# One table of numbers replaced: a second searched order for a fused S4D convolution and Hedgehog attention kernel

## The chip, the core and the metric

The kernel runs on one core of one Trainium2 chip. The metric is the time of one execution in device microseconds (us), as the median of several runs.

## The reference

Two independent layers read their own inputs, and their outputs stand side by side in a (1, 2048, 1152) result. All numbers are float32.

```python
# A: S4D, L=2048, D=576, N=128
dt = exp(log_dt);  A = -exp(log_A_real) + 1j * A_imag
C = (C_real + 1j * C_imag) * dt[:, None]
K = 2 * einsum("dn,dnl->dl", C, exp((A * dt[:, None])[:, :, None] * pos)).real
y = irfft(rfft(u_t, 2 * L) * rfft(K, 2 * L))[:, :, :L]
a = y.transpose(0, 2, 1) + u * D_skip

# B: linear attention, H=32 heads of 18
q, k, v = split(x @ wqkv)
phi = lambda t: concat(softmax(t @ w_phi), softmax(-(t @ w_phi)))     # per head
kv = einsum("bhsf,bhsd->bhfd", phi(k), v);  z = phi(k).sum(s)
o = (phi(q) @ kv) / (phi(q) @ z + 1e-6)
b = o.reshape(B, S, D) @ wo

return concatenate([a, b], axis=-1)
```

## The kernel before

**How the program is put together.** The function `body` does not emit instructions directly. It records 2836 operations through `Plan.op` (a load, a run of matmuls, a copy, an exp, and so on), each with its engine, the operations that it depends on and the buffers that it opens. Then `Plan.run` walks a literal table, `ORDER`, and emits the operations one after another in the order of that table. An entry such as `1250/0/1/7/2/2` says: emit operation 1250 next, and give the buffers that it opens the slots 0, 1, 7, 2 and 2 of their kinds. A star (`268*`) sends an operation that two engines could do to the second of them, and an exclamation mark loads an activation table ahead of need. `7+28` puts 28 filler matmuls at the start. The waits between the engines follow from the table: every engine executes its own instructions in the order in which they were emitted; an operation waits for what it reads and for the earlier readers of a slot that it overwrites. So the table sets two things besides the engine of some operations: who stands behind whom on each engine, and which earlier operation has to be finished before a buffer can be filled again.

**Which buffers there are.** Fourteen large slots serve `zi`, `ac`, `e`, `ks`, `E`; nineteen row slots serve, among others, `ub`, `kb`, `zo`, `fT`, `ot`; there are eight PSUM slots `ps`. All loads and stores that are spoken of below are issued by SP, in order, so that a load which waits for its slot holds back every load and store behind it.

**The work of part B.** All large products run as three products of a high and a low half of the float32 operands (`wh`, `wl` for weights, `x` for tiles). First `fold` multiplies the key weights with the per-head `w_phi`: it loads a block of transposed weights (`e<-in_wkT_dram`, L504) and the `w_phi` block (`fT<-in_wphi_dram`, L500), TensorE multiplies them, ACT writes the high half (`wh<-ps`, L515) and DVE the low half (`wl`, L516). Sixteen key tiles follow (product with `wh`/`wl`, two softmaxes, accumulation of phi(k)ᵀ[v, 1] in the matmuls `ps<-e,v`). Between the last key tiles the same `fold` is done for the query weights (`e<-in_wqT_dram`), of which the first product of a query tile needs every block. Sixteen query tiles then take their softmax, turn the features with nine transposes (`ps<-ident,e`, L701), multiply with kv (`ps<-kvb,fT`) and divide, turn the result (`ps<-ident,o`, L731 and L732) and multiply it with `wo`.

**The work of part A**, interleaved with it. `u_first` does the first stage of the transform of u, 16 times, and stores it (`dram<-zi`, 576 KB). `params` (L845 and after) turns the parameters into exponents and phases in six blocks: its activations need the exp table for `dt<-dt` and the table of the arctangent for `ax<-mn`, and POOL adds integer phases (`pi`, L886). 36 groups build K: products with `sel,mg`, an exp on ACT (L946), products with sines on DVE and POOL (`E`, `cs`, L904, L950 to L956), and 32 small matmuls `ps<-E,cs`. `k_first` stores the first stage of K's transform (`dram<-zi` L989). Sixteen times `product` loads a part of both transforms (`ub<-dram` L1038, `kb<-dram` L1057, a matrix `ff` L1030), makes the products `ub,ff`, `kb,ff` and `ac,ff` on TensorE and stores `zo`; a last stage loads it again as `zi` and makes y.

**The lines in the order's rows and in the trace.** A helper records many operations: L448 is the call of a matmul, L463 and L467 are two-operand operations, L453 a copy. So they are told apart by their tiles. The table is one line shorter after the change, so each line behind it has a number smaller by one there (L448 is L447).

## Time and profile before

| | |
|---|---|
| runs of the kernel before | 512.74, 503.32, 510.81 us; median 510.81 us |
| the profiled execution | 507.23 us; its span 505.4 us |
| instructions in the span | 20522 |
| PE (TensorE matmul) busy | 482.6 us, 95% |
| PEld (TensorE weight load) busy | 404.6 us, 80% |
| DVE, ACT, POOL busy | 454.6 us, 394.9 us, 340.0 us |
| data moved | 115.45 MB, mean 228 GB/s |

The profiled execution is a run of its own, and its 507.23 us lie 1.83 us over the span from its first to its last instruction. A row of the page's groups reads: line, engine, operation, output<-inputs, shapes and count, then the busy time, the mean time of one in ns, and the idle time of the engine ahead of it with what ended it. A row of a timeline reads: start, duration, engine, line, operation, tiles, count, and in brackets how long the engine had been idle ahead of it and what released it. Float32 matmuls count twice in the trace's rows: five of the program stand as x10.

### The profile page before, as it was taken

To read this page: it belongs to the slowest core of one execution; us is meant where nothing else is said; L and a number is where in the kernel's file an instruction comes from. 1 tells how busy PE (TensorE), PEld (TensorE's weight loads), DVE (VectorE), ACT (ScalarE), POOL (GpSimd) and SP (SyncE) were. 2 spreads that over 40 slices of the span, in tenths; PEclk is the share of its full clock that TensorE was granted. 3 is DMA by queue.
4 is the path that set the end of the run, shared out by engine and by line. 5 is a ranking of instruction groups with operands and counts; after the bars stand their busy time and mean duration, and the time that the engine had idled before them with its cause. 6 is when DMAs were issued, how large, how long until landed. Compare 5 with 4: busy or idle time off the path is not lost.

```text
span 505.4 us, 20522 instructions
## 1 busy us (share of the span) xinstructions
PE 482.6 (95%) x8544; PEld 404.6 (80%) x8544; DVE 454.6 (90%) x1010; ACT 394.9 (78%) x684; POOL 340.0 (67%) x413
## 2 busy tenths in 40 slices
PE   6999999999999979899999999998999999998997
PEld 6999988999988768688796877775798786666976
DVE  3999999999999998999998999999898798887684
ACT  5799887999999989998999798999894634444321
POOL 1855789697979996896894799876556327374200
PEclk8999999999999999999999999999999999999999
DMA  8979944822427775567689627878877998999788
GB/s 218 389 239 304 325 146 144 225 81 86 170 69 222 215 237 155 125 217 226 173 270 364 204 67 246 259 242 270 276 251 229 297 291 277 295 284 287 250 303 209
DMA packets 80800, 115.45 MB, mean 228 GB/s; under 512 B 12612, under 2 KB 58564, under 8 KB 80708
## 3 DMA queue, kind: packets, MB, share of 16 engines
q1 hardware_dynamic: 80708, 114.14, 72.2%
q8 instruction: 67, 1.10, 0.9%
q14 instruction: 25, 0.20, 0.1%
HBM read 65.11 MB, written 49.01 MB: 226 GB/s over the span
## 4 chain that ended last, share of the span: by engine, by line
PE 69%; DVE 15%; issue 4%; DMA 4%; POOL 3%; ACT 2%; SPq 1%; DVEq 0%; POOLq 0%; ACTq 0%
PE ps L448 65%; PE ps L701 3%; DVE cs L950 2%; DVE E L467 2%; POOL cs L904 2%; PE ps L731 1%; DVE E L956 1%; DMA kb<-dram 1%; DMA gd<-cs 1%; DVE x L463 1%; DVE E L954 1%; DVE ac L467 1%; DMA ub<-in_wkT_dram 1%; DMA mg<-gd 1%; DVE e L467 1%
## 5 line engine op out<-in xcount | busy, mean ns | idle before, releaser
L448 PE MATMUL ps<-wh,x 128*128 128x288 f32 (+2 forms) x1008 | 241.9, 320 | 0.9 <-DVE e L467 0.4
L448 PEld LDWEIGHTS ps<-wh,x 128*128 128x128 f32 x1008 | 173.4, 188 | 13.2 <-issue 4.8
L448 PE MATMUL ps<-wl,x 128*128 128x288 f32 (+2 forms) x560 | 175.2, 314 | 0.0
L448 PEld LDWEIGHTS ps<-wl,x 128*128 128x128 f32 x560 | 105.5, 188 | 0.2
L904 POOL TENSOR_TENSOR cs<-cs,pi 128x64 int32<-128x64 int32 (+4 forms) x90 | 91.1, 1012 | 4.7
L597 POOL TENSOR_TENSOR o<-e 128x576 f32<-128x576 f32 x32 | 43.0, 1345 | 20.8 <-ACT e L594 16.2
L463 POOL TENSOR_TENSOR E<-v,cs 128x512 f32<-128x512 f32 x34 | 43.6, 1302 | 19.8 <-ACT v L946 19.8
L946 ACT ACTIVATE ps<-ps 128x512 f32<-128x512 f32 x90 | 49.8, 586 | 5.0 <-PE ps L448 4.3
L467 DVE TENSOR_TENSOR ac<-us,ps 128x576 f32<-128x576 f32 x64 | 44.9, 746 | 4.4 <-PE ps L448 2.6
L950 DVE TENSOR_TENSOR cs<-ps,cs 128x1024 f32<-128x1024 f32 x36 | 43.6, 1213 | 1.6 <-ACT ps L946 1.6
L448 PEld LDWEIGHTS ps<-E,cs 128*32 128x32 f32 x2304 | 34.1, 110 | 8.6 <-issue 3.5
L463 POOL TENSOR_TENSOR e<-e,small 128x576 f32<-128x576 f32 x27 | 32.5, 1208 | 12.2 <-DVE small L463 9.5
L922 ACT ACTIVATE cs<-cs,hp 128x1024 f32<-128x1024 f32 x36 | 40.5, 1144 | 0.1
L448 PE MATMUL ps<-E,cs 128*32 128x64 f32 x2304 | 39.2, 220 | 0.9 <-issue 0.4
L594 ACT ACTIVATE e<-e 128x1152 f32<-128x1152 f32 x32 | 37.3, 1167 | 2.6 <-DVE e L463 1.9
L921 ACT ACTIVATE cs<-cs 128x1024 f32<-128x1024 int32 x36 | 37.3, 1054 | 0.2
L886 POOL TENSOR_TENSOR pi<-pi 128x192 int32<-128x192 int32 (+1 forms) x42 | 20.2, 494 | 24.3 <-DVE pi L882 20.2
L463 POOL TENSOR_TENSOR ac<-ac 128x288 f32<-128x288 f32 x31 | 24.2, 808 | 17.5 <-DVE ac L467 17.0
L463 POOL TENSOR_TENSOR e<-small,e 128x576 f32<-128x576 f32 x24 | 28.2, 1174 | 10.7 <-DVE e L467 9.8
L914 ACT ACTIVATE cs<-cs 128x2048 f32<-128x2048 int32 x18 | 34.6, 1922 | 0.5 <-POOL cs L904 0.5
L453 ACT ACTIVATE zi<-ps 128x288 f32<-128x288 f32 x80 | 28.9, 413 | 5.3 <-PE ps L448 5.0
L587 DVE TENSOR_REDUCE small<-ps 128x16 f32<-128x288 f32 (+2 forms) x64 | 28.2, 443 | 4.0 <-PE ps L448 3.7
(143 smaller groups left out, 1013.3 us busy)
## 6 DMA issues: line engine op xcount, KB each, us to landing
dram<-zi SPq DMA_DIRECT2D x32, 288.0 KB, 3.9
xd<-x SPq DMA_DIRECT2D x16, 576.0 KB, 4.1
dram<-zi SPq DMA_DIRECT2D x16, 576.0 KB, 5.6
x<-xd SPq DMA_DIRECT2D x16, 576.0 KB, 4.1
kb<-dram SPq DMA_DIRECT2D x32, 288.0 KB, 4.5
ub<-dram SPq DMA_DIRECT2D x32, 288.0 KB, 4.6
dram<-zo SPq DMA_DIRECT2D x32, 288.0 KB, 4.2
zi<-dram SPq DMA_DIRECT2D x16, 576.0 KB, 7.7
```

Of the source, the lines that this page charges most:

```text
L448: pe.matmul(o, l, r, start=start, stop=stop, skip_group_check=skip)
L453: op(("act", "dve"), (c_act(n), c_dve(n)), lambda e: act.activation(dst(), src(), AF.Copy) if e == "act" else dve.tensor_copy(dst(), src() ...
L463: op(eng, [c_dve(n[0]) if e == "dve" else c_pool(n[1]) for e in eng], lambda e: (dve if e == "dve" else pool).tensor_tensor(dst(), a(), b( ...
L467: op(eng, c_dve(n) if eng == "dve" else c_pool(n), lambda: e.tensor_tensor(dst(), a(), b(), op=alu), r=r, w=w, with_=with_, lock=eng == "p ...
L594: op("act", c_act(1152) + 40, lambda: act.activation(e.t, e.t, AF.Exp), r=[e], w=[e], table="exp")
L597: op("pool", c_pool(517), lambda: pool.tensor_tensor(pair.t, e.t[:, :, :, 0:9], e.t[:, :, :, 9:18], op=ALU.add), r=[e], w=[pair], lock=True)
L904: op("pool", c_add(4 * n * W), lambda n=n, j=j: pool.tensor_tensor(x()[:, :, :, n:2 * n], x()[:, :, :, 0:n], pi.t[:, j:j + 2, gs].bitcast( ...
L914: op(("act", "dve"), (c_act(n) + 45, c_dve(n)), lambda e: act.activation(cs.t[:, 0], x(), AF.Abs) if e == "act" else dve.scalar_tensor_ten ...
L921: op("act", c_act(64 * W) + 150, lambda at=at: act.activation(at(1), at(1).bitcast(I32), AF.Sin, scale=TURN), r=[cs], w=[sine], with_=[cs] ...
L922: op("act", c_act(64 * W) + 225, lambda at=at: act.activation(at(0), at(0), AF.Sin, scale=-TURN, bias=hp.t), r=[cs, hp, sine], w=[both], w ...
L946: op("act", c_act(512) + 12, lambda x=x, y=y: act.activation(y.t, x.t, AF.Exp), r=[x], w=[y], table="exp")
L950: op("dve", c_dve(64 * W), lambda: dve.tensor_tensor(F(), both(M.t), F(), op=ALU.mult), r=[M, ready], w=[long], with_=[cs])
```

## The change

Only the table `ORDER` is different: the same 2836 operations with the same buffers, in another sequence and with other slots, and with some operations on the other of their two engines. Its first two rows:

```diff
-0/0 1 2 234/0 1349 4/1 288/2 1354 1358 1357 1362 1356 1361 1363/3 5/0 7+28/0 1364 1365 1366 1367 1368 1369 1370 6/1
-1355 1359/0 99/4 1371 1360 369/5 1373 1372 19/6 21/2 1374 1375/3 1376 396/7 1377 1378 10 20/3 49/4 12/1 1379 374/8 11
+49/0 5/0 3 0/1 1 2 153/0 1357 1356 4/1 7+28/1 1362 1373 6/2 33 1361 1363/2 1365 1364 1366 1367 1368 72/3 1369 1370
+12/1 1354 1358 35/3 1355 1371 374/4 1372 1359/0 34/4 19/5 1360 1374 14/5 13/6 10 11 369/6 375/1 1375/2 1376 21/1 376*
```

Of the 414 operations that TensorE has, 229 stand at the same place of its sequence, and none moved by more than 15 places. 253 operations run on the second of their engines, before and after. There are 43 loads of an activation table in both, and 376 DMA issues.

**The start, on ACT.** The instructions of the first block of `params` (`dt`, `ay`, `ax`, `pi`), and the first copies of the fold (`wh<-ps`) and of the first tile (`x_193`). Before:

```order
L845 ACT_TABLE_LOAD
L845 ACTIVATE dt<-dt 128x96
L845 ACTIVATE ay<-cim 128x96
L845 ACTIVATE ax<-cre 128x96
L845 ACT_TABLE_LOAD
L845 ACTIVATE ax<-mn 128x96
L845 ACTIVATE ax<-ax 128x96
L861 ACTIVATE pi<-pi 128x96
L845 ACTIVATE ax<-ax 128x96
L515 ACTIVATE wh<-ps 128x126
L543 ACTIVATE x_193<-zo 128x640
```

And now:

```order
L844 ACT_TABLE_LOAD
L844 ACTIVATE ay<-cim 128x96
L844 ACTIVATE ax<-cre 128x96
L844 ACT_TABLE_LOAD
L844 ACTIVATE ax<-mn 128x96
L844 ACTIVATE ax<-ax 128x96
L844 ACT_TABLE_LOAD
L844 ACTIVATE dt<-dt 128x96
L844 ACTIVATE ax<-ax 128x96
L860 ACTIVATE pi<-pi 128x96
L514 ACTIVATE wh<-ps 128x126
L542 ACTIVATE x_193<-zo 128x640
```

The exponential of `dt` and a third table load now stand between the arctangent (`ax<-mn`) and the first copy of the folded weights. On SP the loads of the start changed places too: the first key weights (`e<-in_wkT_dram`) were the fifth load and are the first, `fT<-in_wphi_dram` was the first and is the fourth, and `dt` was the second and is the seventh.

**The fold of the query weights, on PE.** `fT,e` are the fold's products, `sel,mg` and `E,cs` belong to the groups of K, `e,v` accumulates a key tile (its number is that of the tile's `v`). Before:

```order
L448 MATMUL ps<-sel,mg 128x256 x6
L448 MATMUL ps<-e,v_2509 19x36 x32
L448 MATMUL ps<-fT,e 128x126 x8
L448 MATMUL ps<-e,v_2715 19x36 x32
L448 MATMUL ps<-sel,mg 128x256 x6
L448 MATMUL ps<-fT,e 128x126 x5
L448 MATMUL ps<-E,cs 32x64 x32
```

And now:

```order
L447 MATMUL ps<-sel,mg 128x256 x6
L447 MATMUL ps<-e,v_2178 19x36 x32
L447 MATMUL ps<-fT,e 128x126 x5
L447 MATMUL ps<-sel,mg 128x256 x6
L447 MATMUL ps<-e,v_1523 19x36 x32
L447 MATMUL ps<-fT,e 128x126 x9
L447 MATMUL ps<-E,cs 32x64 x32
```

Before, the fourth block of query weights (operation 518, `e<-in_wqT_dram`) was loaded into a slot whose last reader stood seven operations ahead of its product on PE. Now it is loaded into the slot that the `fT,e ... x5` above has just read, and its product is in the `fT,e ... x9`, with a `sel,mg`, an `e,v` and the five products of the third block between them. On SP, the loads around it, before:

```order
L774 DMA dram<-zi 64x1152
L504 DMA e<-in_wqT_dram 126x640
L989 DMA dram<-zi 128x8x144
L491 DMA e<-in_wo_dram 128x960
L504 DMA e<-in_wqT_dram 126x640
L989 DMA dram<-zi 128x8x144
L504 DMA e<-in_wqT_dram 126x640
L554 DMA x_3273<-xd 128x1152
```

And now:

```order
L773 DMA dram<-zi 64x1152
L503 DMA e<-in_wqT_dram 126x640
L838 DMA dt<-in_ldt_dram 128x96
L503 DMA e<-in_wqT_dram 126x640
L988 DMA dram<-zi 128x8x144
L490 DMA e<-in_wo_dram 128x960
L503 DMA e<-in_wqT_dram 126x640 x2
L553 DMA x_3286<-xd 128x1152
```

The third and the fourth block (operations 511 and 518) are issued one behind the other, where a store stood between them. The slot of the third was last read by the 576 KB store of a `k_first` (L988 here).

**The transposes of query tile 9, on PE.** `ident,o` turns that tile's divided output, `ident,e` turns the features of another tile, `ub,ff` and `ac,ff` are of a `product`, `kvb,fT` of a query tile. Before:

```order
L448 MATMUL ps<-ub,ff 32x288 x16
L701 MATMUL ps<-ident,e 128x128 x5
L448 MATMUL ps<-sel,mg 128x256 x6
L701 MATMUL ps<-ident,e 128x128 x4
L731 MATMUL ps<-ident,o 128x128 x4
L732 MATMUL ps<-ident,o 128x128
L448 MATMUL ps<-ac,ff 32x288 x32
```

And now:

```order
L447 MATMUL ps<-ub,ff 32x288 x16
L730 MATMUL ps<-ident,o 128x128 x4
L731 MATMUL ps<-ident,o 128x128
L700 MATMUL ps<-ident,e 128x128 x4
L447 MATMUL ps<-sel,mg 128x256 x6
L700 MATMUL ps<-ident,e 128x128 x4
L447 MATMUL ps<-kvb,fT 64x76 x4
```

The turn of the output went ahead of the other tile's turns and of the group's `sel,mg`; products `kvb,fT` went ahead of `ac,ff`.

**Two smaller places.** Ahead of the first query tile's transposes, three phase adds (`pi`, L886) on POOL went out from in front of the multiplication `e<-e,small` (L463) of that tile. And for `product` 15 the second of the two loads of `kb` (L1057, operations 2706 and 2707) waits for the reader of another slot: before, for the product `kb,ff` of `product` 10, now for its product `ub,ff`, which stands one operation earlier on PE.

## The prediction

> **What bounds the kernel now.** I read the page's busy times first, then TensorE's own waits, then the windows around the largest of them. The page's first part, and the two rows of its chain and groups that bear on the bound:

> ```profile
> span 505.4 us, 20522 instructions
> PE 482.6 (95%) x8544; PEld 404.6 (80%) x8544; DVE 454.6 (90%) x1010; ACT 394.9 (78%) x684; POOL 340.0 (67%) x413
> PE 69%; DVE 15%; issue 4%; DMA 4%; POOL 3%; ACT 2%; SPq 1%; DVEq 0%; POOLq 0%; ACTq 0%
> L448 PE MATMUL ps<-wh,x 128*128 128x288 f32 (+2 forms) x1008 | 241.9, 320 | 0.9 <-DVE e L467 0.4
> ```

> TensorE is busy for 482.6 us of 505.4, so 22.8 us of idle time are all that another order can take from it as long as its matmuls cost the same. An order changes no matmul: the counts are equal, and 320 ns is what one of the largest group takes wherever it stands. DVE is second with 454.6; the chain gives it 15% against PE's 69%, so it is close behind in places, but it has 505.4 − 454.6 = 50.8 us of slack over the whole. Here is what TensorE waits for (engine, line, releaser: us in total, times, longest):

> ```profile
> PE ps L448 <- issue: 5.7, 7, 1.9
> PE ps L448 <- DMA e<-in_wkT_dram: 1.9, 1, 1.9
> PE ps L731 <- ACT ps L946: 1.6, 1, 1.6
> PE ps L226 <- DVE dsk L998: 1.6, 1, 1.6
> PE ps L701 <- POOL e L463: 1.5, 1, 1.5
> PE ps L448 <- DMA kb<-dram: 1.0, 1, 1.0
> PE ps L448 <- DVE wl L516: 1.0, 1, 1.0
> ```

> These seven rows make 14.3 us, and each row but the first is one wait at one place. 5.7 us are "issue", waits for nothing that the profile shows; nothing in the rows lets me call them a property of the order, so I leave them as they are. The others are the waits of this particular order. The question is which of them the new order removes, which it keeps, and which it makes. Much of the sequence is the same on PE (229 of 414 operations at the same place), so I go through the places where a wait stood, and through the shortest distances between a load and its use in the new order.

> **Term 1, the start.** The timeline of the first microseconds (start, duration, engine, operation; in brackets the idle time before and its releaser):

> ```profile
> 2.60 0.47 SPq L504 DMA_DIRECT2D e<-in_wkT_dram  x1
> 4.17 0.28 ACT L845 ACTIVATE dt<-dt 128x96 f32<-128x96 f32 x1 [2.15 <-DMA dt<-in_ldt_dram]
> 6.45 1.35 PE L448 MATMUL ps<-fT,e 126*128 126x126 f32 x10 [1.90 <-DMA e<-in_wkT_dram]
> 6.86 1.28 ACT L845 ACT_TABLE_LOAD   x1 [1.50 <-DVE mn L467]
> 8.16 0.28 ACT L845 ACTIVATE ax<-mn 128x96 f32<-128x96 f32 x1
> 9.56 0.26 ACT L515 ACTIVATE wh<-ps 128x126 fp32r<-128x126 f32 x1
> 10.79 0.74 ACT L543 ACTIVATE x<-zo 128x640 fp32r<-128x640 f32 x1 [0.98 <-PE ps L448]
> ```

> The first product waits for the key weights, the fifth load, issued at 2.60 and there at 6.45, 3.85 us later. The new order issues them first and the other operand `fT` fourth, so the later of the two leaves one place sooner; an issue takes SP 0.47, which makes −0.5. Against that, the exponential of `dt` (0.28) and a table load (1.28 at 6.86) now stand between the arctangent and the first copy `wh<-ps`; before, `dt` was done at 4.17 in ACT's idle time. In the two engines' terms: the matmuls start at about 5.9 instead of 6.45, the copy at about 9.56 + 1.28 + 0.28 − 0.3 (the parameters land a little sooner too) = 10.8. Behind the first copy ACT had 0.98 us of idle time, which takes that much of the 1.26: 0.3 us remain, and another 0.1 for the copies that are bunched behind it. I take **+0.4**. From below, if the copies have slack, the earlier weights show at TensorE, −0.5, and with a table load less in the way of the first tile −0.9; from above the whole 1.56 shows.

> [...]

> **Term 2, the fold of the query weights.** TensorE's and SP's rows there:

> ```profile
> 175.60 0.34 SPq L504 DMA_DIRECT2D e<-in_wqT_dram  x1
> 175.90 0.75 PE L448 MATMUL ps<-e,v 128*19 128x36 f32 x64
> 176.62 2.02 PE L448 MATMUL ps<-fT,e 126*128 126x126 f32 x16
> 179.41 0.50 PE L448 MATMUL ps<-sel,mg 32*128 32x256 f32 x6
> 180.87 1.38 PE L448 MATMUL ps<-fT,e 126*128 126x126 f32 x10 [0.96 <-DVE wl L516]
> 189.19 0.78 PE L448 MATMUL ps<-fT,e 72*128 72x72 f32 x5 [1.88 <-issue]
> ```

> Before, the fourth block's load left at 175.60 and its product ran at 180.87, 5.27 us later, with 0.96 us of waiting. In the new order its slot comes free with the product that precedes it by a `sel,mg` (0.50), an `e,v` (0.75) and five `fT,e` (1.38): 2.63 us of work on TensorE. That is the shortest distance from a slot's release to its use that I find in the new sequence; by the same row durations the next is 4.95, and the shortest of the old one was 4.39. How long such a load takes no row says alone: the same shape at the start landed 3.85 us after its issue, a loaded queue has longer:

> ```profile
> kb<-dram SPq DMA_DIRECT2D x32, 288.0 KB, 4.5
> dram<-zi SPq DMA_DIRECT2D x16, 576.0 KB, 5.6
> ```

> A load of 288 KB lands after 4.5 us in the median; 315 KB at that rate after 4.9. So the wait is 3.85 − 2.63 = 1.2 to 4.9 − 2.63 = 2.3; with about 0.2 for the release and the issue, 1.4 to 2.5. In its place the old 0.96 for `wl` goes, as the later load covers it: +0.4 to +1.5, and I take **+1.0**, the middle. TensorE's queue holds behind this wait the `E,cs` of a group and the remaining products of the fold, so all of it shows.

> There is a worse end. The third block's slot was read by a 576 KB store, which lands 5.6 us after its issue, and SP issues the fourth load behind the third. If the store lands late, both loads leave late, and then 2.63 us of work cover nothing: the fourth block would be needed at the same time, and 4.9 us pass from its issue, less 0.6 of the matmuls already there: +4.3. By the sequence the store is out early enough that I do not take this end; it is a rival below.

> The 1.88 us of "issue" at 189.19 stand between matmuls of one operation, so that no order of operations removes them; that speaks for leaving the 5.7 us in place.

> **Term 3, POOL ahead of the first query tile's turns.**

> ```profile
> 201.41 1.68 POOL L886 TENSOR_TENSOR pi<-pi 128x192 int32<-128x192 int32 x3
> 201.68 1.17 ACT L594 ACTIVATE e<-e 128x1152 f32<-128x1152 f32 x1
> 203.05 2.76 POOL L597 TENSOR_TENSOR o<-e 128x576 f32<-128x576 f32 x2
> 206.54 1.16 POOL L463 TENSOR_TENSOR e<-e,small 128x576 f32<-128x576 f32 x1
> 207.76 1.20 PE L701 MATMUL ps<-ident,e 128*128 128x128 f32 x9 [1.46 <-POOL e L463]
> ```

> TensorE waits 1.46 us for a chain on POOL, from which the new order takes the three phase adds (1.68 us). But the sums `o<-e` behind them need the exp of ACT, which ends at 201.68 + 1.17 = 202.85, and they started at 203.05: only 0.2 of the 1.68 was in the way. **−0.2**, with −1.5 as the end where the whole wait goes.

> **Term 4, the transposes of query tile 9.**

> ```profile
> 338.53 1.20 PE L448 MATMUL ps<-ub,ff 64*32 64x288 f32 x32
> 339.01 0.41 DVE L467 TENSOR_TENSOR o<-ps,small 128x252 f32<-128x252 f32 x1
> 340.36 0.52 PE L448 MATMUL ps<-sel,mg 32*128 32x256 f32 x6
> 342.23 0.62 ACT L946 ACTIVATE ps<-ps 128x512 f32<-128x512 f32 x1
> 343.10 0.60 PE L731 MATMUL ps<-ident,o 128*128 128x128 f32 x4 [1.64 <-ACT ps L946]
> ```

> The turn of `o` waits for PSUM: its slot is given back when ACT has done the exp of the `sel,mg` ahead of it (342.23 + 0.62 = 342.85). Its input was ready at 339.01 + 0.41 = 339.42. Now it stands right behind `ub,ff`, at about 339.7, and ahead of that `sel,mg`; the wait has no cause left. But TensorE then reaches the exp's other customers 1.6 us sooner, and some of it comes back: between −1.6 and 0, I take **−1.0**.

> **Term 5, the last loads of `kb`.**

> ```profile
> 438.70 0.87 SPq L1057 DMA_DIRECT2D kb<-dram  x2
> 444.40 0.78 PE L448 MATMUL ps<-kb,ff 32*32 32x288 f32 x32 [0.99 <-DMA kb<-dram]
> ```

> The second load's slot now comes free one operation sooner on TensorE, and that operation is a `kb,ff` of 0.78 us: the load leaves 0.7 to 0.8 sooner and the wait of 0.99 shrinks by it, **−0.7** (−1.0 to 0, if the full queue takes it away).

> **The rest.** The tail (two query tiles' last products and their stores) has the same form and is costed at 0. DVE gets about 4 us less of copies and ACT about 3 more; under DVE's 50.8 us of slack and ACT's 505.4 − 394.9 = 110.5 nothing of it shows, and if that cover were gone the price would be those 3 to 4 us. The other waits in the list stay.

> **The sum:** 0.4 + 1.0 − 0.2 − 1.0 − 0.7 = −0.5 us, against the profiled execution's own 507.23 (1.83 over its span), which makes 506.7. That execution lies 3.6 us under the median of the runs, 510.81, and I cannot tell which of them another day will be like; I take the middle of the two, 509.0, as the level, and forecast **508.5 us**. Adding the low ends of the terms gives −0.9 + 0.4 − 1.5 − 1.6 − 1.0 = −4.6, the high ends 1.56 + 1.5 = +3.1; with the half of the runs' spread (12.74 − 3.32) / 2 = 4.7 combined as independent, the case's own range is 502 to 514.

> **The rivals.** *The waits go without return.* TensorE's end has the form of before, and its idle time there (the row of the last window: length, then PE's busy time) stays:

> ```profile
> 500.00:505.40 5.40, 1.80 (x14) 1.57 (x12) 0.46 (x1) 0.39 (x1) 0.00 (x0) 1.00 0.67 202
> ```

> Of the 22.8 us, 5.40 − 1.80 = 3.6 are at the end, 5.7 "issue", and 1.9 and 1.6 at the start. The remaining 10.0 are waits for other engines and loads, all made by the old order. If the new one has them all filled, the time is 509.0 − 10.0 = 499.0. For it speaks that terms 3 to 5 each take away the cause of a named wait; against it that over half of TensorE's operations stand where they stood and keep their neighbours, and that a TensorE that is sooner meets the next late engine.

> *The late query weights.* SP holds the third and the fourth block behind one slot (term 2's worse end), and everything SP issues behind them, the next tile's `x<-xd` first, leaves as late. With +4.3 once and the start at +1.56: 509.0 + 4.3 + 1.6 = 514.9, slower than before; with the same delay paid a second time at the gemm that needs `x`, 519.2. It decides from the point where that store lands less than 4.9 us ahead of the third block's product, so that both loads are late together. For it speaks that DMA is at 0.88 of its engines in that stretch; against it that on SP another load (`in_wo`) stands between the store and the third block:

> ```profile
> 180.00:190.00 10.00, 7.25 (x226) 6.44 (x227) 8.55 (x20) 8.05 (x13) 9.61 (x10) 1.00 0.88 275
> ```

> *Nothing changes but places.* Each wait removed comes back at the next engine, and each new one replaces an old one: 509.0. It lies inside the forecast's own range and I do not separate it.

> **How the numbers follow.** The forecast, with the last rival in it, has 0.66; the waits that go 0.17; the late weights 0.17. About 2%, 10.2 us, is what a measurement of this kernel can tell from no change: faster is below 500.6, slower above 521.0. Of the first rival's 0.17, six tenths lie below 500.6 (its 499.0 is 1.6 under it), 0.10, and 0.03 come from the forecast's lower tail: 0.13 faster. Of the second's 0.17, about half lie above 521, where 519.2 and the runs' half spread of 4.7 reach, 0.09, and 0.03 come from the forecast's upper tail: 0.12 slower. 0.75 remain for the same. The range 499 to 520 leaves out some 0.09 below and 0.11 above.

> **What would show it.** At the start, the first `ps<-fT,e` at about 5.9 and the first `wh<-ps` copy near 10.8, the first product `wh,x` a little later than before's. Near 180 us a wait of 1.4 to 2.5 us of TensorE for `e<-in_wqT_dram`, where none was. No wait at the turn `ident,o` behind `ub,ff` near 340, and one of some 0.3 us or none for `kb<-dram` in the last 70 us. TensorE's busy time again near 482.6, its idle time 20 to 25 us. I am wrong if PE's busy time moves by more than 3 us, if a wait of over 3 us stands at one place, or if the "issue" rows, which I left alone, change by more than 2 us.

## The result, and the profile after

| | median | runs |
|---|---|---|
| before | 510.76 us | 503.32 to 512.74, four runs |
| after | 522.03 us | 520.85 to 523.53, four runs |

The ratio is 1.0269, with a 95% interval of 1.0221 to 1.0317: slower, the medians lie 11.3 us apart, and the time is outside the forecast's 499 to 520. The profiled execution took 520.85 us. Ratios here leave out runs that a lower clock made several us longer, so they are not quite quotients of the medians, and two profiles further down, those of a_shift and a_late_wo, are of such runs: of these I use where a wait stands and how long it is, not their totals.

The page's first part after the change, the row of the granted clock, the chain by engine and the largest group:

```profile
span 519.0 us, 20548 instructions
PE 488.9 (94%) x8544; PEld 410.2 (79%) x8544; DVE 454.1 (87%) x1010; ACT 397.8 (77%) x689; POOL 339.9 (65%) x409
PEclk8999999989999998999999999998999999999999
PE 68%; DVE 15%; ACT 6%; issue 6%; DMA 4%; SPq 1%; POOL 0%; DVEq 0%; ACTq 0%
L447 PE MATMUL ps<-wh,x 128*128 128x288 f32 (+2 forms) x1008 | 245.1, 323 | 4.8 <-DVE cs L949 1.9
```

The span grew by 519.0 − 505.4 = 13.6 us. TensorE's busy time grew by 488.9 − 482.6 = 6.3 us with the same 8544 matmul records, and its idle time from 22.8 to 30.1 us, by 7.3. So nearly half of the loss is in matmuls that took longer. The clock row says where: it has four slices of 8, where before's has only the first:

```profile
PEclk8999999999999999999999999999999999999999
```

The windows around these slices, after the change (window, length, busy time of PE, PEld, DVE, ACT, POOL with counts, granted clock, DMA share, GB/s):

```profile
7.81:14.63 6.82, 6.82 (x34) 6.66 (x32) 3.05 (x10) 5.14 (x13) 0.90 (x1) 0.50 0.98 296
106.80:110.21 3.41, 3.41 (x44) 2.95 (x46) 3.41 (x6) 0.37 (x1) 0.88 (x1) 0.50 0.01 3
202.37:205.78 3.41, 3.41 (x17) 3.41 (x15) 1.50 (x6) 2.55 (x5) 0.00 (x0) 0.50 0.06 19
359.38:362.79 3.41, 3.41 (x70) 2.26 (x81) 2.27 (x4) 2.12 (x2) 1.10 (x1) 0.50 0.03 9
```

And the only such stretch before:

```profile
7.67:11.08 3.41, 3.03 (x15) 2.89 (x14) 2.10 (x8) 1.95 (x7) 0.00 (x0) 0.50 1.00 273
```

17.05 us at half clock against 3.41: half of the difference, 6.8 us, is lost work, which is the 6.3 us of busy time and a little in the gaps between. The stretches stand on one grid: 106.80 − 7.81 = 29 × 3.41, 202.37 − 106.80 = 28 × 3.41, 359.38 − 202.37 = 46 × 3.41, and (359.38 − 7.81) / 103 makes the step 3.413 us. Ahead of each one TensorE had been idle, and these are its waits in the changed kernel:

```profile
PE ps L447 <- issue: 7.3, 5, 4.1
PE ps L447 <- DMA fT<-in_wphi_dram: 2.2, 1, 2.2
PE ps L700 <- DVE x L466: 1.9, 1, 1.9
PE ps L447 <- DVE cs L949: 1.9, 1, 1.9
PE ps L447 <- DVE ks L466: 1.6, 3, 0.8
PE ps L226 <- DVE zero L482: 1.6, 1, 1.6
PE ps L447 <- ACT ax L844: 1.4, 1, 1.4
```

Where the four that cost clock stand, by the timelines:

```profile
6.81 1.56 PE L447 MATMUL ps<-fT,e 126*128 126x126 f32 x10 [2.20 <-DMA fT<-in_wphi_dram]
105.69 0.45 PE L447 MATMUL ps<-wh,x 128*128 128x396 f32 x1 [1.89 <-DVE cs L949]
201.82 0.60 PE L447 MATMUL ps<-fT,e 72*128 72x72 f32 x4 [4.08 <-issue]
359.05 0.84 PE L700 MATMUL ps<-ident,e 128*128 128x128 f32 x4 [1.93 <-DVE x L466]
```

Before had a wait of 1.88 us too, at 189.19, without loss of clock. It lay from 187.31 to 189.19, and before's grid (7.67 + 53 × 3.413 = 188.56) cuts it into 1.25 and 0.63. The 1.89 us ahead of 105.69 lie whole between 103.39 and 106.80. The wait of 1.59 us that ended at 194.55 lies whole between 192.1 and 195.5 and cost no clock. So in this trace 1.59 us of idle time inside one step of the grid did not lose the clock and 1.89 did, and a loss, 3.41 us at a granted clock of 0.50, takes 3.41 / 2 = 1.7 us of work from TensorE. Over the sixteen kept traces the line is less sharp. Of the steps at full clock with over 1.8 us without a matmul, 38 of 40 were followed by a half clock; with 1.2 to 1.8 us 12 of 49 were, and none with less. The two exceptions, 1.92 us in a_late_wo and 1.89 us in a_shift, are shown below.

To see where the loss arises I compare the times at which TensorE begins its n-th matmul record; the count is the same in both kernels and their products differ little in place. All numbers are differences to the profiled execution of before, in us:

| n | 78 | 300 | 1150 | 1300 | 2600 | 3140 | 3400 | 8300 | end |
|---|---|---|---|---|---|---|---|---|---|
| before, at | 14.35 | 48.22 | 96.93 | 108.90 | 174.98 | 203.38 | 216.55 | 477.77 | 505.44 |
| after | +2.5 | +4.8 | +3.0 | +7.0 | +8.5 | +14.0 | +14.0 | +13.1 | +13.6 |

Three places carry it: the start (+3.0 at n = 1150), the product of a key tile at 105 us (+4.0 from 1150 to 1300), and the fold of the query weights (+5.5 from 2600 to 3140). From 217 us to the end the new order is in sum level with the old one.

**The refills.** The "issue" waits and some with another name have one thing in common. Count all of TensorE's instructions in the trace together: the matmuls, the weight loads, and the 199 semaphore and drain instructions between them (197 after the change). Then these waits end where an instruction of number 193 + 256 k is due: 5825, 6081, 11457, 11713, 11969 in one kernel or in both. Two are at the same count in both kernels, 6081 and 11969, though different operations stand there. Each ends 1.25 to 1.5 us after the end of a packet of 16 KB on the instruction queue, of which the page counts the same number as before, one for every 258 of TensorE's 2 × 8544 + 197 = 17285 instructions:

```profile
q8 instruction: 67, 1.10, 0.8%
```

For three of these, from the trace's packets and matmuls (us):

| instruction | kernel | block ahead entered | packet starts | packet takes | TensorE goes on | idle |
|---|---|---|---|---|---|---|
| 5825 | before | 179.03 | 180.78 | 1.22 | 183.74 | none |
| 5825 | after | 188.07 | 192.29 | 0.96 | 194.55 | 1.59 |
| 6081 | before | 183.74 | 186.74 | 1.02 | 189.19 | 1.88 |
| 6081 | after | 194.55 | 199.40 | 1.00 | 201.82 | 4.08 |
| 11969 | before | 336.79 | 340.65 | 1.08 | 343.10 | 1.64 |
| 11969 | after | 352.53 | 356.40 | 1.15 | 359.05 | 1.93 |

Behind the first three blocks, the packet of a block starts after TensorE has entered the block ahead in 58 of 63 blocks in each kernel, and up to 1.6 us before it in the others. From these times I infer, and no row shows it directly, that a packet is asked for about there and then waits its turn among the data of the DMA engines; the runs below bear the second out only in part. If the block runs out before its packet is there, TensorE stands still, as in the table's column of idle time. Added up, waits of over 0.25 us at such a count are 1.88 + 0.40 + 1.64 + 0.74 + 0.81 + 1.45 = 6.9 us before, and 0.29 + 1.59 + 4.08 + 1.08 + 0.77 + 1.93 = 9.7 after.

At the fold SP's rows after the change show what that packet met:

```profile
190.77 0.32 SPq L503 DMA_DIRECT2D e<-in_wqT_dram  x1
192.90 0.80 SPq L553 DMA_DIRECT2D x<-xd  x2
193.75 0.43 SPq L988 DMA_DIRECT2D dram<-zi  x1
194.22 0.79 SPq L665 DMA_DIRECT2D kz<-kvb  x1
195.21 1.14 SPq L490 DMA_DIRECT2D e<-in_wo_dram  x1
```

Two loads of 576 KB, a store of 576 KB and the 480 KB of `in_wo` leave within 3 us, right where block 5825 is entered (194.55). The packet for 6081 starts 4.85 us after that.

### The profile page after: what moved, and what is told of

Its sections match the earlier page's. It is cut to its first block, busy times and chain, and to the rows that moved or that the text cites. A ratio compares the mean times of both kernels' runs of the same rounds, so it can differ in the third digit from the quotient of the medians.

```text
span 519.0 us, 20548 instructions
## 1 busy us (share of the span) xinstructions
PE 488.9 (94%) x8544; PEld 410.2 (79%) x8544; DVE 454.1 (87%) x1010; ACT 397.8 (77%) x689; POOL 339.9 (65%) x409
## 4 chain that ended last, share of the span: by engine, by line
PE 68%; DVE 15%; ACT 6%; issue 6%; DMA 4%; SPq 1%; POOL 0%; DVEq 0%; ACTq 0%
PE ps L447 64%; PE ps L700 3%; DVE cs L949 2%; PE ps L730 1%; DMA dram<-zi 1%; ACT ps L945 1%; DVE x L462 1%; DMA cim<-in_cim_dram 1%; DVE E L953 1%; DVE ac L466 1%; DVE ks L466 1%; DMA fT<-in_wphi_dram 1%; DVE e L466 1%; DVE E L955 1%; ACT cs L921 1%
## 5 line engine op out<-in xcount | busy, mean ns | idle before, releaser
L447 PE MATMUL ps<-wh,x 128*128 128x288 f32 (+2 forms) x1008 | 245.1, 323 | 4.8 <-DVE cs L949 1.9
L462 POOL TENSOR_TENSOR E<-v,cs 128x512 f32<-128x512 f32 x33 | 42.1, 1292 | 8.6 <-ACT v L945 8.6
L462 POOL TENSOR_TENSOR e<-e,small 128x576 f32<-128x576 f32 x28 | 33.7, 1203 | 11.1 <-DVE small L462 10.2
L462 POOL TENSOR_TENSOR e<-small,e 128x576 f32<-128x576 f32 x25 | 29.8, 1193 | 16.2 <-DVE small L462 11.9
L452 ACT ACTIVATE zi<-ps 128x288 f32<-128x288 f32 x87 | 31.0, 412 | 10.2 <-PE ps L447 10.2
L447 PEld LDWEIGHTS ps<-kvb,fT 128*64 128x64 f32 x640 | 25.0, 139 | 8.5 <-issue 2.0
## 6 DMA issues: line engine op xcount, KB each, us to landing
dram<-zi SPq DMA_DIRECT2D x32, 288.0 KB
xd<-x SPq DMA_DIRECT2D x16, 576.0 KB
dram<-zi SPq DMA_DIRECT2D x16, 576.0 KB
x<-xd SPq DMA_DIRECT2D x16, 576.0 KB
kb<-dram SPq DMA_DIRECT2D x32, 288.0 KB
ub<-dram SPq DMA_DIRECT2D x32, 288.0 KB
dram<-zo SPq DMA_DIRECT2D x32, 288.0 KB
zi<-dram SPq DMA_DIRECT2D x16, 576.0 KB
```

The lines of the kernel that those rows point to most:

```text
L447: pe.matmul(o, l, r, start=start, stop=stop, skip_group_check=skip)
L452: op(("act", "dve"), (c_act(n), c_dve(n)), lambda e: act.activation(dst(), src(), AF.Copy) if e == "act" else dve.tensor_copy(dst(), src() ...
L462: op(eng, [c_dve(n[0]) if e == "dve" else c_pool(n[1]) for e in eng], lambda e: (dve if e == "dve" else pool).tensor_tensor(dst(), a(), b( ...
```

## The experiments

The profile explains the time with two things that the forecast did not have: refills that, as I read it, wait behind data, and idle time that costs clock. The rival explanation is that of the forecast's own steps: late loads and slots, each worth its length. Eight kernels change one thing in the new order or in the old one, four carry the new order in one stretch of TensorE's operations alone, and two change two or three things together. Ratios are to the kernel before on the same chip, with 95% intervals. Table rows as above, in us against the profiled execution of before:

| n | 78 | 1150 | 1300 | 2600 | 3140 | 3400 | end |
|---|---|---|---|---|---|---|---|
| a_swap | +3.8 | +5.0 | +7.1 | +9.4 | +16.5 | +16.6 | +17.5 |
| a_late_x | +4.4 | +6.3 | +10.3 | +11.8 | +16.9 | +16.9 | +18.6 |
| a_start | +1.9 | +5.7 | +9.8 | +11.3 | +16.5 | +16.7 | +17.1 |
| b_start48 | +4.2 | +6.9 | +7.1 | +8.6 | +10.2 | +10.2 | +11.3 |
| b_start66 | +4.3 | +5.5 | +9.5 | +11.4 | +12.4 | +12.4 | +12.5 |
| b_fold | +0.8 | +0.4 | +0.5 | +1.6 | +6.7 | +5.6 | +11.5 |
| b_rest | 0.0 | 0.0 | 0.0 | 0.0 | +4.8 | +9.4 | +9.4 |
| b_traffic | +1.3 | −0.6 | −0.6 | −0.3 | +2.5 | +2.5 | +4.4 |
| b_fill | +0.6 | −1.2 | −1.1 | −0.8 | +1.0 | +1.0 | +4.1 |
| a_fill | +1.5 | +1.9 | +4.5 | +6.3 | +11.7 | +11.7 | +9.9 |
| a_fill_swap | +1.7 | +2.2 | +4.3 | +6.6 | +10.9 | +11.0 | +9.7 |
| a_mend | +1.7 | +2.2 | +6.3 | +8.1 | +13.2 | +13.6 | +11.7 |

**a_swap: the key tile's product at 105 us.** In the new order, operation 165 (the product of key tile 4) stands behind the `sel,mg` of two groups, which take six PSUM slots, so that it waits for `cs`; the accumulation 265 stands behind it. Here 265 goes ahead.

```diff
-165/6 265 424
+265 165/6 424
```

> The changed kernel with one swap: the accumulation of key tile 7 (matmuls e,v, 0.75 us) stands ahead of the product of key tile 4 that waited 1.89 us for PSUM at 105.7 us. Theory, the waits are priced by the clock too: the wait falls to about 1.1 us, under what brings the half clock, the 3.41 us at half clock behind it go, and the time falls by 0.8 + 1.7 = 2.5 us against the changed kernel. Rival, a wait costs its own length and the half clock is not its doing: the wait falls to 1.1 us, a stretch at half clock of 3.41 us stays near 107 us, and the time falls by 0.8 us.

Measured: 523.79 us, ratio 1.026 [1.0184, 1.0335]. The wait of 1.89 became two short ones:

```profile
107.00 0.25 PE L446 MATMUL ps<-e,v 128*19 128x36 f32 x6 [0.55 <-issue]
107.71 0.45 PE L446 MATMUL ps<-wh,x 128*128 128x396 f32 x1 [0.46 <-DVE cs L948]
```

No half clock stands at that place, and from 1150 to 1300 it lost 2.1 us instead of 4.0. So the cause of that loss is right. The time did not fall by the 2.5 us that I expected, which is a miss: the start was 2 us later, and the fold cost 7.1 us instead of 5.5, with refills of 2.37 us at 196.48 and 3.09 us at 204.36 and a half clock behind each.

**a_late_x: fewer transfers ahead of the refill.** The two loads of `x<-xd` (619 and 1009) go behind the small stores and loads of the key sums, right ahead of the operation that needs the first of them.

```diff
-619/12 1009/1 520/1
+520/1
...
-485 1270/1/2/3/0/9 620/6
+485 1270/1/2/3/0/9 619/12 1009/1 620/6
```

> The changed kernel with two loads of x tiles (576 KB each) issued by SP behind the store of zi and that of kz at about 195 us, where they stood ahead of them at 192.9 us. Theory, the 4.08 us of issue at 201.8 are TensorE's instruction refill, whose packet waits behind data: with 1.15 MB less in flight when the refill is asked for, its packet starts 2 to 4 us sooner, the wait falls under 2 us, no half clock follows, and the time falls by 3 to 6 us. Rival, the wait belongs to the last block of the fold, in whose products it stands: it stays at 4 us and so does the time, within 1 us.

Measured: 522.89 us, ratio 1.0263 [1.0198, 1.0328]. The refill at the 72-wide products shrank from 4.08 to 2.44 us, and the one ahead of it grew:

```profile
199.10 0.62 PE L446 MATMUL ps<-e,v 128*19 128x36 f32 x49 [2.45 <-issue]
204.72 0.90 PE L446 MATMUL ps<-fT,e 72*128 72x72 f32 x4 [2.44 <-issue]
```

The step lost 5.1 us instead of 5.5, against the 3 to 6 that I expected to gain: the size is a miss. The packet for 6081 did start sooner, 3.31 us after the block ahead was entered instead of 4.85, but that for 5825 later, 4.77 instead of 4.22.

**a_start: the start of before.** The first 84 operations stand in before's sequence.

```diff
-49/0 5/0 3 0/1 1 2 153/0 1357 1356 4/1 7+28/1 1362 1373
+0/1 1 2 4/1 1354 1358 1357 1362 1356 1361 1363/2 5/0 7+28/4
```

> The changed kernel with the sequence of the kernel before for its first 84 operations (the loads of the start, the exponential of dt ahead of the arctangent, the 72-column block of the fold third instead of second). Theory: the first product wh,x starts at about 14.5 us instead of 16.9, one stretch of 3.41 us at half clock at the start instead of two, and the time falls by about 2.4 us. Rival, that the start's lateness is taken up by the slack behind it: the first product starts at 14.5 us and the time stays within 0.5 us.

Measured: 524.57 us, ratio 1.0284 [1.023, 1.0339]; a miss. The first product `wh,x` came at 16.22 instead of 16.88, but at 50 us the wait for ACT grew from 1.45 to 2.29 us and took the clock with it:

```profile
50.77 0.65 PE L446 MATMUL ps<-wh,x 128*128 128x378 f32 x1 [2.29 <-ACT ax L843]
```

0.65 instead of the 0.41 of the same matmul in the changed kernel. TensorE came to this wait only 0.2 us sooner than there, and the wait ended 0.65 later, so most of its growth is ACT's.

**a_shift: the same order, 128 instructions later.** 64 tiny matmuls with zeros follow the fillers, so that every block of 256 ends at another operation.

```diff
+            for _ in range(64 if not o[12] else 0):
+                self.matmul(t[0:32, 0:8], self.zero.t[0:32, 0:32], self.data.t[0:32].bitcast(BF16)[:, 0:8], start=True, stop=True)
```

> The changed kernel with 64 very small matmuls of zeros (8 columns) behind the 28 filler matmuls at the start, so that every later instruction of TensorE stands 128 places further in its stream. Theory, the issue waits are refills of 256 instructions each: they stay at the same places of the stream (counted in TensorE's instructions) and so move to other operations, 128 instructions earlier in the program: the 4.08 us inside the 72-column products of the fold are gone from there. Also TensorE is busy while it waits for the first weights, so the half clock at the start is shorter by a stretch or two of 3.41 us, 1.7 us each. Rival, the waits belong to the operations: they stay in the 72-column products, at the transposes behind query tile 9's and at the same E,cs. The time is not forecast by either but for the start, -1.7 to -3.4 us by the theory; refills at other places can give or take 4 us.

Measured: 527.72 us, ratio 1.033 [1.0246, 1.0414]. The wait at the 72-wide products is gone, and it stands in the `E,cs` ahead of them:

```profile
199.15 0.91 PE L448 MATMUL ps<-E,cs 128*32 128x64 f32 x49 [1.89 <-issue]
```

That is the end of instruction block 6081 again, now 128 instructions earlier in the program. No engine and no load has to do with these `E,cs`; the place goes with the count. This is what shows the "issue" waits to be refills. Over the sixteen traces all of them over 0.15 us but three (0.17, 0.28 and 0.36 us) end at such a count. Why this one is 1.89 us long instead of 4.08 the run does not show. It cost no clock, though it lies inside one step of the grid. The start was a miss: its half clock, from 8.36 to 15.19, is as long as in the changed kernel.

**b_start48, b_start66, b_fold, b_rest: the changed order in one stretch.** Before's table, with TensorE's operations 0 to 48, 0 to 66, 105 to 136, or 136 to the end (and what they depend on) in the changed sequence. Slots had to be given anew at the seams, and in the first three also behind the stretch, at 585, 577 and 314 entries up to the end; this is the weakness of the four. Beginnings of the stretches:

```diff
-0/0 1 2 234/0 1349 4/1 288/2 1354 1358 1357 1362 1356 1361 1363/3 5/0 7+28/0
+49/0 5/0 3 0/1 1 2 1357 1356 4/1 7+28/1 1362 1373 6/2 33 1361 1363/2
...
-1320/2/5/1/3/11 504/3 505/6 93! 94/0 1619* 1322 506/5
+1268 1619* 93 1320/5/2/3/1/0 1323 504/3 506/6 1815*
...
-1659/4/2/5/7/1 537 1174 1660 1655/6 1015
+1227/4 853/1 1275 1174 1659/6/4/5/8/7 1015
```

> The kernel before with the changed sequence for TensorE's first 48 operations (up to about 95 us) and everything of the other engines between them; the rest as before. Theory, the loss is made in a few places (the profiles stand 3.0 us apart at the end of this stretch, 7.0 at TensorE's operation 66, 5.5 more behind the fold of the query weights, and 0.4 less at the end): 3 us slower than before. Rival, the loss is spread over the program: this stretch is a fifth of the span, 2 to 3 us of the 13.6. The two differ in the next one.

> The kernel before with the changed sequence for TensorE's first 66 operations (up to about 109 us), so with the product of key tile 4 that waits behind two groups' sel,mg. Theory: 7 us slower than before, with a wait of some 1.9 us at 105 us and 3.41 us at half clock behind it. Rival, spread: 3 us slower.

> The kernel before with the changed sequence for TensorE's operations 105 to 136 alone (the fold of the query weights, about 172 to 204 us), the fourth block's load in the slot that the fold's product ahead has just read. Theory: TensorE's refill waits grow there to 4 us or more in one place, a half-clock stretch follows, and the time rises by 5 us. Rival, the forecast's own term, the late load of the fourth block alone: a wait for that load of 1 to 2.5 us and 1 us in all.

> The kernel before with the changed sequence for TensorE's operations from 136 on (from about 204 us to the end, 60% of the span). Theory: 0.4 us faster than before, within 1.5 us of it. Rival, spread: 8 us slower.

Measured, in this order: 517.91, 519.49, 518.26 and 517.22 us; ratios 1.0121 [1.0073, 1.017], 1.0156 [1.0113, 1.0199], 1.0118 [1.0062, 1.0174] and 1.012 [1.0081, 1.0159]. Every part is slower than before by about as much as the others: by the medians 6.4, 8.0, 6.8 and 5.7 us, where the theory had 3, 7, 5 and −0.4.

The start alone costs 6.9 us at n = 1150, more than in the whole change. The first products show why; in b_start48:

```profile
9.22 2.25 PE L447 MATMUL ps<-fT,kvb 72*128 72x72 f32 x10
11.26 2.43 PE L447 MATMUL ps<-fT,e 126*128 126x126 f32 x10
16.42 2.47 PE L447 MATMUL ps<-fT,e 126*128 126x126 f32 x10 [0.59 <-PE ps L447]
```

Ten `fT,e` take 2.43 to 2.47 us, against 1.35 in before's first product and 1.42 in the changed kernel's last, and 2.43 at 10.20 in its stretch at 0.50: by these durations everything ran at half clock until past 18 us. (A window there reads a clock of 1.00, since the trace's first record of the clock starts at 20.42 in this run; I go by the durations.) The changed kernel itself was at full clock from 14.63 in its profiled run.

In b_start66 the wait for `cs` is back, now that the stretch reaches to operation 165, and the step from 1150 to 1300 costs +3.9 (+4.0 in the whole change), where b_start48 lost 0.2:

```profile
108.19 0.45 PE L447 MATMUL ps<-wh,x 128*128 128x396 f32 x1 [1.91 <-DVE cs L949]
```

In b_fold the fourth block of weights, which the forecast's second term had, is late, and its products wait:

```profile
179.56 0.34 SPq L503 DMA_DIRECT2D e<-in_wqT_dram  x1
183.40 1.00 ACT L530 ACTIVATE wh<-e 128x960 fp32r<-128x960 f32 x1 [3.71 <-DMA e<-in_wo_dram]
184.31 1.55 ACT L945 ACTIVATE ps<-ps 128x512 f32<-128x512 f32 x3
184.92 1.22 DVE L949 TENSOR_TENSOR cs<-ps,cs 128x1024 f32<-128x1024 f32 x1 [2.87 <-ACT ps L945]
186.20 2.08 PE L447 MATMUL ps<-fT,e 126*128 126x126 f32 x8 [2.88 <-DVE cs L949]
```

And the window of the clock:

```profile
185.87:189.28 3.41, 3.08 (x49) 2.86 (x53) 3.26 (x6) 3.41 (x5) 1.59 (x2) 0.50 0.11 24
```

The products that waited are the fourth block's, 6.64 us after its load was issued. But the trace has that load landed at 184.65, which accounts for 1.3 of the 2.88 us. The rest is the wait that the profile names: the products' PSUM slot came free with `cs` at 186.14, whose exp on ACT stood behind a copy that had waited 3.71 us for `in_wo`. 2.88 us and a half clock: the amount is that of my theory (+5.1 at the fold), but no refill waited there, and of the rival's mechanism, the late load, only a part is there.

For b_rest I expected nothing, and it lost 9.4 us: 4.8 in the part that it shares with before, where the refill at the 72-wide products happened to be 2.97 us long (1.88 before, in the same order) and cost two windows of clock, and 4.6 at its seam, with waits of 1.42 and 3.37 us. From there to the end it lost nothing.

```profile
191.23 1.13 PE L446 MATMUL ps<-fT,e 72*128 72x72 f32 x4 [2.97 <-issue]
```

The window of these two steps of the clock:

```profile
190.70:197.50 6.80, 6.27 (x36) 5.13 (x37) 2.81 (x9) 2.81 (x6) 2.46 (x2) 0.50 0.35 137
```

What follows: start, 105 us and fold each cost by themselves, and the parts do not add up. By medians 8.0 (0 to 66) + 6.8 (fold) + 5.7 (rest) = 20.5 us against the 11.3 of the whole.

**b_traffic: more data ahead of the refill, in the old order.** Two loads of 576 KB that nothing reads, in front of the next tile's load (525).

```diff
-525/7 1780
+2836 2837 525/7 1780
```

> The kernel before with two more transfers of 576 KB that nobody waits for (from an input to a scratch in memory), issued by SP ahead of the last block of query weights at about 182 us. Theory, the issue waits are refills of TensorE's instructions whose packet waits behind data: the wait of 1.88 us in the 72-column products of the fold (matmul 3015 of TensorE's stream) grows by 2 to 4 us, a half-clock stretch follows it, and the time rises by 3 to 6 us. Rival, that wait is the fold's own (its products' operands or PSUM): it stays at about 1.9 us; a later load of weights or x would be named as a wait for that load, and the time rises by less than 2 us.

Measured: 513.09 us, ratio 1.007 [1.004, 1.0099]; +2.7 us from 2600 to 3140.

```profile
189.66 1.31 PE L447 MATMUL ps<-fT,e 72*128 72x72 f32 x10 [2.76 <-DMA e<-in_wqT_dram]
```

The size is as the theory had it, but the wait stands at the first of the ten products and not inside them, and it is the weights' own load that came late behind the extra ones. It speaks rather against the theory: the packet for 6081 started 3.43 us after the block ahead was entered, where before's took 3.00, so 1152 KB more ahead of it moved it by 0.4 us.

**b_fill, a_fill, a_fill_swap: keeping TensorE busy until the first product.** The 28 fillers go onto operation 6, whose tile is wider, and are 220 columns wide instead of 126; a_fill_swap has the edit of a_swap too.

```diff
-            n = min(256, t.shape[1])
+            n = min(220, t.shape[1])
...
-7+28/1 1362 1373 6/2
+6+28/2 7/1 1362 1373
```

> The kernel before with the 28 filler matmuls at the start made 220 columns wide instead of 126, so that TensorE stays busy until about 6.7 us, when the first weights land. Theory, TensorE's idle 1.9 us ahead of the first product lets the clock fall to a half: the first product wh,x starts at 13 us instead of 14.35 and the time falls by 1 to 2 us. Rival, that stretch is covered by the loads behind it: no change.

> The changed kernel with the same wider fillers. Theory: the clock stays full from about 8 us on instead of being at a half until 14.6 to 20.6 us (as the profiles of the changed start show it), the first product wh,x starts at about 14 us instead of 16.9 to 18.8, and the time falls by 2.5 to 4.5 us against the changed kernel. Rival, that the copies on ACT behind the extra table load set the start: first product at 16 us, time 0 to 1 us less.

> The changed kernel with the wider fillers and the swap of the accumulation of key tile 7 ahead of key tile 4's product. Theory, the two are independent: 2 us less than the changed kernel with the fillers alone at TensorE's matmul 1300 (about 112 us), and 0 to 2 us less at the end, since refills behind it can take it back. Rival, the swap is worth nothing also at 112 us.

Measured: 511.5 us, ratio 1.0057 [1.0026, 1.0088]; 518.92 us, 1.0194 [1.0142, 1.0245]; 521.21 us, 1.0219 [1.0172, 1.0267]. In the old order it lost 0.6%, where a gain of 1 to 2 us was expected. The start ran at full clock there by its durations (the first ten `fT,e` took 1.35 us), but the first product `wh,x` came at 14.97 instead of 14.35, since TensorE now waited for a load that the half clock had covered, as the rival had it:

```profile
12.27 1.08 PE L447 MATMUL ps<-fT,kvb 72*128 72x72 f32 x8 [1.35 <-DMA kvb<-in_wkT_dram]
```

In the new order the wait ahead of the first product was 1.11 us instead of 2.20, and the start ran at full clock, with 1.32 to 1.35 us for ten products:

```profile
7.12 1.35 PE L446 MATMUL ps<-fT,e 126*128 126x126 f32 x10 [1.11 <-DMA fT<-in_wphi_dram]
9.38 1.32 PE L446 MATMUL ps<-fT,e 126*128 126x126 f32 x10
12.41 1.35 PE L446 MATMUL ps<-fT,ub 126*128 126x126 f32 x10 [1.71 <-DMA ub<-in_wkT_dram]
104.62 0.45 PE L446 MATMUL ps<-wh,x 128*128 128x396 f32 x1 [1.89 <-DVE cs L948]
```

And the window behind that last wait:

```profile
104.60:108.00 3.40, 3.38 (x78) 3.11 (x78) 3.40 (x5) 1.25 (x4) 2.02 (x1) 1.00 0.24 80
```

The first product `wh,x` came at 15.87 instead of 16.88 (14 expected), since a load shows here too, and the kernel is 1.9 us behind at n = 1150 rather than 3.0 to 6.3. Whether the time fell by the 2.5 to 4.5 us expected is not shown: the ratio is 1.0194 against 1.0269, on another chip and with intervals that overlap. The last row of the timeline and the window are the sharpest evidence that the grid decides: the same wait of 1.89 us as in the changed kernel, at nearly the same time, and the clock stayed at 1.00. By the trace's records a step of this run's grid begins at 4.96, so another at 4.96 + 29 × 3.413 = 103.94, which cuts the wait (102.73 to 104.62) into 1.21 and 0.68 us. With that, a_fill_swap had nothing to gain at 105 us and gained nothing of the 2 us expected: +4.3 at n = 1300 where a_fill has +4.5.

**a_late_wo: the store and the `in_wo` load behind the refill.** 1621 (the 576 KB store) and 535 (`in_wo`) go behind 492; by the trace they are issued at 205.61 and 206.34 instead of 193.75 and 195.21.

```diff
-1621 1169/3
+1169/3
...
-535/2 1010/4 492 495
+1010/4 492 1621 535/2 495
```

> The changed kernel with a store of zi (576 KB) and a load of output weights (480 KB) issued by SP behind the store of kz at about 207 us, where they left at 193.75 and 195.2 us; two loads of x stay at 192.9. Theory, refill behind data: the wait in the 72-column products falls from 4.08 us to 1 to 2.5 us, and between TensorE's matmuls 2600 and 3140 the changed kernel loses 2 to 3.5 us on the one before where it lost 5.5. What the late store costs behind 207 us is not forecast (its buffer is wanted by query tile 2), so the end is open. Rival, the loss there is that of the fold's own operands: it stays between 5 and 6 us.

Measured: 524.09 us, ratio 1.0215 [1.0139, 1.0292]. The refill of 6081 is 1.89 us long instead of 4.08, and costs no clock; the one ahead of it, which meets the same traffic as before, is 1.92 instead of 1.59:

```profile
195.74 0.62 PE L446 MATMUL ps<-e,v 128*19 128x36 f32 x49 [1.92 <-issue]
200.82 0.60 PE L446 MATMUL ps<-fT,e 72*128 72x72 f32 x4 [1.89 <-issue]
```

The step from 2600 to 3140 is +3.6 (expected +2 to +3.5). In the six profiled kernels with the changed order there and nothing moved at it (the changed kernel, a_swap, a_start, a_fill, a_fill_swap, a_mend) that wait is 3.09 to 4.36 us, in a_late_x 2.44. So what SP sends ahead of the packet takes part in that wait's length; it is not alone in it, since in before's order the same count has 0.65 to 2.97 us. The 1.92 us at 195.74 lie inside one step of the grid (192.64 to 196.05) and cost no clock either. The time did not gain; why is not shown.

**a_mend: fillers, swap, and two copies on ACT moved** (1473 and 1514 behind 263), to take the wait at 50 us away as well.

```diff
-1473 251/2 250 252/10 1514 69/5
+251/2 250 252/10 69/5
...
-263 1505/1
+263 1473 1514 1505/1
```

> The changed kernel with the wider fillers, the swap at 105 us, and on ACT two copies of v out of PSUM ahead of a sine and an arctangent at 48.7 us. Theory: no wait of 1.45 us at 50 us; at TensorE's matmul 1300 the changed kernel is 0.5 to 3 us behind the one before where it was 7.0; at the end 515 to 518 us, the fold's loss being left. Rival, the first 110 us are not where the loss is made: time as with the fillers alone or the changed kernel, 519 to 522 us.

Measured: 520.11 us, ratio 1.0171 [1.0104, 1.0238]. The wait at 50 us kept its length and changed its name, so the two copies were not its cause; and the refill at 105 us took the place of the wait for `cs`:

```profile
49.32 0.41 PE L446 MATMUL ps<-wh,x 128*128 128x378 f32 x1 [1.46 <-DVE e L465]
105.72 0.27 PE L446 MATMUL ps<-e,v 128*19 128x36 f32 x6 [2.13 <-issue]
```

A miss: +6.3 at n = 1300 where 0.5 to 3 were expected. None of the kernels beats the one before.

**The three places over all the profiles.** The table's differences show which loss goes with the order and which with the execution. The start, at n = 1150: +1.9 to +6.9 in the nine kernels with the changed order up to there, −1.2 to +0.4 in the four others. The place at 105 us, from 1150 to 1300: 3.9 to 4.2 us with the changed order (a_mend, where a refill took the place, among them), 2.1 to 2.5 in a_swap, a_fill and a_fill_swap, which kept the clock there, and 0.2 at most with before's order. The fold, from 2600 to 3140: 4.3 to 7.1 us with the changed order; with before's order and no traffic added 1.0, 1.6, 1.8 and, in b_rest, 4.8. So the first two losses are clear of the scatter between executions, and part of the fold's 5.5 us is that before's profiled execution was a good one there.

## Why the prediction was wrong

**The step that failed** is the second paragraph's: "An order changes no matmul: the counts are equal, and 320 ns is what one of the largest group takes wherever it stands", together with "nothing in the rows lets me call them a property of the order, so I leave them as they are" on the 5.7 us of "issue". The first sentence made every wait worth its own length; the runs showed that a wait of some 1.9 us or more may cost TensorE 1.7 us of work more, by where it falls on the clock's grid (6.8 us in the profiled execution). The second left refills out; they grew by 2.8 us, in part with the transfers that SP now sends when a packet is due (a_late_wo). What remains of the 13.6 us by subtraction, some 4, is waits for engines and loads. The text's own conditions for being wrong, PE's busy time off by more than 3 us and a wait of over 3 us at one place, were both met (6.3 and 4.08). That no order removes a wait between matmuls of one operation did not hold: at the same count the wait was 4.08 us in the changed kernel, and in b_fold there was none.

**Term 1, the start: +0.4, measured +2.5** at the first product `wh,x` (16.88 against 14.35). `fT` as the fourth load left at 2.14, 0.46 us sooner as forecast, but took 4.67 us instead of 3.85 and was there at 6.81, not at 5.9, so TensorE waited 2.20 instead of 1.90 us; the clock fell for two windows instead of one, 1.7 us more. The copy of `wh` came at 11.30 against the 10.8 that I gave. ACT's part was about right; what failed is the load's time, which the forecast kept as it was, and the clock. They do not simply add: a_fill, at full clock, still began `wh,x` 1.5 us late, so by that run the clock has 1.0 of the 2.5. The changed kernel's profile even shows a mild start: a_swap and a_late_x, which begin alike, are at +3.8 and +4.4 there.

**Term 2, the late fourth block: +1.0, and the place cost +5.5.** In the changed kernel TensorE waited only 0.45 and 0.18 us at these products, and for ACT and DVE, not for the load. Both sizes of the term were off: by the trace the load left at 186.97 and had landed at 190.06, 3.1 us later (3.85 to 4.9 were taken), and TensorE reached its product at 190.65, 3.7 us after the load's issue (2.63 were taken). The 0.2 us for the release and the issue was an estimate that no row stood for; the issue began 0.03 us after the matmul that freed the slot (186.94). The 5.5 us came behind these products, with refills of 1.59 and 4.08 us and 1.7 of clock. The load can be late, as in b_fold, where it landed 5.1 us after its issue; it alone accounts for 1.3 us there, just under the 1.4 to 2.5 given, and the half clock was not priced. The rival of the late query weights, with 514.9 to 519.2, had the place, SP's row of loads at the fold, and the sign; its price came from the wrong customer.

**Term 3, POOL ahead of the first query tile: −0.2, measured −0.7**: the wait is 0.74 instead of 1.46 us at 221.64. A small miss in my favour.

**Term 4, the turn of `o` at query tile 9: −1.0, measured about +2.** The profile named ACT's exp for the 1.64 us, and the order did take that reason away. But the wait ended at instruction 11969, 1.37 us after its packet had landed; the exp had been done only 0.25 us sooner, so two causes stood behind one wait. The new order meets the same count with 1.93 us, named for DVE, whose result was there 1.0 us before the wait ended, and loses a window of clock. A releaser that the profile names is the last event that fits, not always the cause.

**Term 5, the loads of `kb`: −0.7**, right: the wait of 0.99 is gone from the list.

**What was missed altogether:** the product of key tile 4 at 105 us (+4.0). I looked for short distances between a load and its use; this is a short distance between six PSUM slots taken by `sel,mg` and the next operation that needs one. Before, an `e,v` (0.75 us) and one more product `wh,x` stood between. The table of the order shows this as well as the loads.

**What stays open.** How much each place has in the median's 11.3 us: a half clock depends on where the grid stands in an execution (a wait of 1.89 us at 105 us cost it in the changed kernel and not in a_fill), and kernels with the same start lie between +3.0 and +6.9 at n = 1150. Before's profiled execution is 3.5 us below its own median, so the 13.6 us hold some luck. Why the new start loses the clock for longer than the old one is only argued: its second operation is the 72-wide block, whose matmuls are shorter (2.25 us for ten in b_start48, against 2.43 of the 126-wide); a_start, which puts it back, had its clock sooner (eight `fT,e` in 1.06 us at 10.43), but is one kernel. That data in front of the packet lengthens a refill is borne out at one place, by a_late_wo, in a single profile; b_traffic, which added data, moved the packet by only 0.4 us. The order at least goes with it: in the eight other profiled kernels whose order there is the changed one the packet for 5825 starts 3.67 to 5.12 us after the block ahead is entered, in the six with before's 1.49 to 1.86 us. No kernel undid it without losing elsewhere.

## What to carry to other kernels

On a TensorE that is busy 95% of the time, price a wait by its length and by the clock that it may cost (here 1.7 us for each step at 0.50), and do not leave the "issue" rows aside: count instructions, and see which transfers leave while the next block of 256 is due. Before believing a releaser, look whether the wait ends at such a count and, as here, 1.25 to 1.5 us after the end of an instruction packet; and before disbelieving one, look when the other suspect was done, as with the load in b_fold. A new order of the same operations can lose at each place where it puts transfers or slots close together (+5.5 us at the fold, +4.0 at 105 us), and it gained nothing in sum where the waits were refills (6.9 us before, 9.7 after), one of which came back under another name (at instruction 11969, 1.64 us before and 1.93 after).
